# A first batch that is transposed on chip: an FFT filter and an MLP with ELU on one core

## The chip, the cores and the metric

The kernel runs on one core of a Trainium2 chip. The core has five engines that run side by side and wait for each other through semaphores: TensorE (PE in the profile; its weight loads are PEld), VectorE (DVE), ScalarE (ACT), GpSimd (POOL) and SyncE (SP), which only issues transfers here. Sixteen DMA engines move data between DRAM and the on-chip memory (SBUF); TensorE writes its results to a small memory of eight banks (PSUM), from which VectorE or ScalarE copies them. The metric is the device time of one execution in microseconds (us). Less is better.

## What is computed

Each of 8 batches of 3008 rows of 256 numbers goes through a real Fourier transform along the rows, is multiplied by a complex filter, and is transformed back. All rows then go through an MLP of width 2048 with ELU.

```python
X = np.fft.rfft(x, axis=1)                     # x: (8, 3008, 256) float32
y = np.fft.irfft(X * F[None], n=3008, axis=1)  # F = filt_r + 1j*filt_i, 1505 x 256
h = y.reshape(24064, 256) @ w_in               # 256 x 2048
g = np.where(h > 0, h, np.exp(np.minimum(h, 0)) - 1)
return g @ w_out                               # 2048 x 256
```

The weights w_in and w_out reach the kernel as 64-bit floats, 4.2 MB each, and are converted to 32-bit ones on the chip.

## The kernel before

3008 is 47 x 64, so the transform is made of two factors. Stage A contracts the 64 values of one index (with the pair n1 and 47 - n1 folded together), stage B the 47 values of the other. B's result is multiplied by the filter, and two more stages (Bi and N) go back. Then the MLP follows in items of one (batch, block m, quarter q), made with a Strassen-like scheme of 7 products up (w_in) and 7 down (w_out). Batches overlap: while the MLP of one batch fills TensorE, the transform of the next is slipped in. Only for the first batch there is no MLP to hide the transform behind. This is the part concerned.

Stage A leaves its rows in the wrong partitions for stage B. So its result t goes to a DRAM tensor z and comes back in another order.

```python
def x_unit(b, c):                 # c = 0..5: one block of 4 rows and their mirror rows
    nc.vector.tensor_tensor(out=u, in0=t[:, 0], in1=t[:, 1], op=ALU.add)
    nc.vector.tensor_tensor(out=t[:, 1], in0=t[:, 0], in1=t[:, 1], op=ALU.subtract)

def a_unit(b, c):                 # 16 matmuls of 64 x 64, two evictions
    ...
    nc.scalar.activation(out=t[:, 0:2, :], in_=p0, func=AXT.Copy)
    nc.scalar.activation(out=t[:, 2:4, :], in_=p1, func=AXT.Copy)

def z_write(b, c):                # 256 KB each, 1 KB runs
    ...
    for r in range(2):
        nc.sync.dma_start(z[r], t[HALVES[r]])

def z_read(b, g):                 # g = 0..7: one group of 4 frequencies
    for p, r in enumerate((0, 24, 64, 88)):
        nc.sync.dma_start(t[r:r + 24]..., zs[b][:, k:k + 4, :]...)
```

Stage B of a group, the product with the filter (the four VectorE lines are L251 to L254 of the profile), and stage Bi, whose result goes to DRAM (yd) and comes back for stage N:

```python
def b_unit(b, g, f=None):
    ...                                            # 4 matmuls of 512 columns
    nc.vector.tensor_tensor(out=sr, in0=re, in1=f[:, 0], op=ALU.mult)
    nc.vector.tensor_tensor(out=si, in0=re, in1=f[:, 1], op=ALU.mult)
    nc.vector.tensor_tensor(out=p, in0=im, in1=f[:, 1], op=ALU.mult)
    nc.vector.tensor_tensor(out=q, in0=im, in1=f[:, 0], op=ALU.mult)
    nc.gpsimd.tensor_tensor(out=sr, in0=sr, in1=p, op=ALU.subtract)
    nc.gpsimd.tensor_tensor(out=si, in0=si, in1=q, op=ALU.add)

def bi_unit(b, g):                                 # 4 matmuls, then two copies
    ...
    nc.scalar.activation(out=t[:, 0:2, :], in_=pa, func=AXT.Copy)
    nc.scalar.activation(out=t[:, 2:4, :], in_=pb, func=AXT.Copy)
```

The weights come in 16 pieces k (k = 4q + j; j = 0, 1 of w_in, j = 2, 3 of w_out), 0.5 MB each. A piece is fetched as pairs of 32-bit words and converted in one go: mantissa and exponent are taken apart, made floats, and joined.

```python
def w_convert(k):
    nc.vector.tensor_scalar(out=m, in0=hi, scalar1=0x000FFFFF, op0=ALU.bitwise_and, ...)
    nc.scalar.activation(out=l, in_=lo, func=AXT.Identity, scale=2.0 ** -52)
    nc.scalar.activation(out=f, in_=m, func=AXT.Identity, scale=2.0 ** -20, bias=1.0)
    nc.vector.tensor_scalar(out=e, in0=hi, scalar1=20, scalar2=0x7FF, ...)     # shift, and
    nc.vector.tensor_scalar(out=e, in0=e, scalar1=1151.0, scalar2=896.0, ...)  # min, max
    nc.vector.tensor_scalar(out=e, in0=e, scalar1=896.0, scalar2=8388608.0, ...)
    nc.vector.scalar_tensor_tensor(out=e, in0=hi, scalar=0x80000000, in1=e, ...)
    nc.vector.tensor_tensor(out=f, in0=f, in1=l, op=ALU.add)
    ... # one product (j < 2) or two half ones into the weight tile
    if j % 2 == 1:
        ... # four VectorE additions of 128 x 256 between the tile's blocks
```

The start, in program order:

```python
for c in range(NXC):                  # 6
    x_load(0, c, ...)                 # 6 (5 for c = 0) transfers on SP, one table on ACT
nc.gpsimd.memset(ff, 0.0)
... # tables; pieces 2 and 3
for a in range(2):
    f_read_first(ff, a)               # the filter of all groups, on GpSimd's queue
for c in range(NXC):
    x_unit(0, c); a_unit(0, c); z_write(0, c)
    if c in (0, 2): w_convert(c // 2)
for k in range(4, 7): w_fetch(k)
for k in range(2, 6): w_convert(k); w_fetch(k + 5)
z_read(0, 0); z_read(0, 1)
for g in range(NG + 2):               # 10
    if g >= 2: bi_unit(0, g - 2)
    if g < NG: b_unit(0, g, ff[:, g]); ...   # z_read(0, g + 2)
    if g >= 2: y_write(0, g - 2)
    if g in CONVERTS: w_convert(CONVERTS[g]) # {1: 6, 3: 7, 5: 8, 7: 9, 8: 10, 9: 11}
    ...
y_read(0, 0); w_convert(12)
... # fetch 13, 14, 15, each converted later between the first MLP items
n_unit(0, 0)
```

Of the kernel before, what the change touches and what calls it, by code (L numbers as in the profile page):

```python
# [10 lines left out]
FP32 = mybir.dt.float32  # L11
# [29 lines left out]
def _make_tables():  # L41
# [9 lines left out]

    n2, k2 = np.arange(N2), np.arange(K2)
    ta, tn = np.zeros((P, H, P)), np.zeros((P, H, P))
    for i in range(H):
        for h in range(2):
            if h and i == 0:
                continue
            n1 = N1 - i if h else i
            th = 2 * np.pi * (((N1 * n2[:, None] + n1) * k2[None]) % N) / N
            c, s = np.cos(th), -np.sin(th)  # L60
            c[:, 0], s[:, 0] = 1.0, 1.0 - 2.0 * (n2 % 2)
            sign = -1.0 if h else 1.0
            r = slice(h * 64, h * 64 + 64)
            for p, v in enumerate((c, sign * s, s, sign * c)):
                ta[r, i, p * 32:p * 32 + 32] = v
                tn[p * 32:p * 32 + 32, i, r] = v.T
    tb = ta.reshape(2, 2, 32, NXC, 2, 2, 4, 16, 2)[:, 0].transpose(3, 0, 1, 2, 4, 7, 5, 6)
# [24 lines left out]
    return [t.astype(np.float32) for t in (ta, tn, gb, gr, gi)]  # L92
# [8 lines left out]
def kernel(  # L101
# [11 lines left out]
    ta_d, tn_d, gb_d, gr_d, gi_d = [  # L113
        nc.inline_tensor(t, name=n).ap() for t, n in zip(_make_tables(), ("ta_t", "tn_t", "gb_t", "gr_t", "gi_t"))
# [28 lines left out]
    junk = glob.tile([P, 1], FP32, name="junk")  # L143
    fd = fdp.tile([NG, 2, 48, 2, 2, D], FP32, name="fd")
# [56 lines left out]

    def z_write(b, c):
# [18 lines left out]
    def f_read_first(t, a):  # L221
# [3 lines left out]
        for c, src in enumerate((filt_r, filt_i)):  # L225
            nc.gpsimd.dma_start(t[r:r + 24, :, c, :, :].rearrange("q g u d -> q g (u d)"),
                                raw(src, 2 * a, [[64 * D, 24], [4 * D, NG], [1, 2 * D]]))
            for u in range(2):
                g0 = 1 if a == u == 0 else 0
                for r0, n in ((24, 16), (40, 7)):  # L230
                    nc.gpsimd.dma_start(t[r + r0:r + r0 + n, g0:NG, c, u, :],
                                        raw(src, 64 * (r0 - 23) - 4 * g0 - 2 * a - u,
                                            [[64 * D, n], [-4 * D, NG - g0], [1, D]]))
            if a == 0:
                nc.gpsimd.dma_start(t[24:48, 0, c, 0, :], raw(src, 32, [[64 * D, 24], [1, D]]))
# [5 lines left out]
    def b_unit(b, g, f=None):  # L241
# [236 lines left out]
    wbufs = list(fbufs)  # L478

    def w_fetch(k):  # L480
        q, j = divmod(k, 4)

        wd = wds[k] = wbufs[k % 5 if k < 12 else (2, 0, 1, 2)[k - 12]].bitcast(U32).rearrange("p c u d -> p (c u d)").rearrange("p (a w) -> p a w", w=2)
# [8 lines left out]
    def w_convert(k):  # L492
# [3 lines left out]
        q, j = divmod(k, 4)  # L496
        if j < 2:
            dst = w_in[q][:, 2 * j:2 * j + 2, :, :].rearrange("p j a c -> p a j c")
            shape = dict(a=2, j=2)
        else:  # L500
            dst = w_out[q][:, 0:4, j - 2, :]
            shape = None
        wd = wds.pop(k)
        lo, hi = wd[:, :, 0], wd[:, :, 1]
        m, e = (kp.tile([P, 512], U32, tag=t, name=n) for t, n in (("k0", "wm"), ("k1", "we")))
        fl = kp.tile([P, 2, 512], FP32, tag="c", name="wfl")
        f, l = fl[:, 0], fl[:, 1]

        nc.vector.tensor_scalar(out=m, in0=hi, scalar1=0x000FFFFF, scalar2=None, op0=ALU.bitwise_and)
        nc.scalar.activation(out=l, in_=lo, func=AXT.Identity, scale=2.0 ** -52)  # L510
        nc.scalar.activation(out=f, in_=m, func=AXT.Identity, scale=2.0 ** -20, bias=1.0)

        nc.vector.tensor_scalar(out=e, in0=hi, scalar1=20, scalar2=0x7FF,
                                op0=ALU.logical_shift_right, op1=ALU.bitwise_and)
        nc.vector.tensor_scalar(out=e, in0=e, scalar1=1151.0, scalar2=896.0, op0=ALU.min, op1=ALU.max)
        nc.vector.tensor_scalar(out=e, in0=e, scalar1=896.0, scalar2=8388608.0,
                                op0=ALU.subtract, op1=ALU.mult)
        nc.vector.scalar_tensor_tensor(out=e, in0=hi, scalar=0x80000000, in1=e,
                                       op0=ALU.bitwise_and, op1=ALU.bitwise_or)
        nc.vector.tensor_tensor(out=f, in0=f, in1=l, op=ALU.add)  # L520
        if shape:
            f, e = (t.rearrange("p (a j c) -> p a j c", **shape) for t in (f, e.bitcast(FP32)))
        else:

            f, e = (t.rearrange("p (i a e s) -> p i e a s", i=2, a=4, e=2) for t in (f, e.bitcast(FP32)))
            dst = dst.rearrange("p (i e) (a s) -> p i e a s", i=2, a=4)
        if shape:
            nc.vector.tensor_tensor(out=dst, in0=f, in1=e, op=ALU.mult)
        else:
            for i in range(2):  # L530
                nc.vector.tensor_tensor(out=dst[:, i], in0=f[:, i], in1=e[:, i], op=ALU.mult)
        if j % 2 == 1:
            w = (w_in if j < 2 else w_out)[q]
            a11, a21, a12, a22, s1, s2, s4 = (w[:, i] for i in range(7))
            nc.vector.tensor_tensor(out=s1, in0=a21, in1=a22, op=ALU.add)
            nc.vector.tensor_tensor(out=s2, in0=s1, in1=a11, op=ALU.subtract)
            nc.vector.tensor_tensor(out=s4, in0=a12, in1=s2, op=ALU.subtract)
            nc.vector.tensor_tensor(out=a21, in0=a11, in1=a21, op=ALU.subtract)
# [19 lines left out]
    with tc.manual_schedule():  # L558


        CONVERTS = {1: 6, 3: 7, 5: 8, 7: 9, 8: 10, 9: 11}
        with tc.tile_pool(name="boot", bufs=1) as bp:
            ff = bp.tile([P, NG, 2, 2, D], FP32, name="ff")
            wbufs += [bp.tile([P, 2, 2, D], FP32, name="wb%d" % i) for i in range(2)]
            more = [(bp.tile([P, 2, 2, D], FP32, name="xb%d" % i), bp.tile([P, 2, P], FP32, name="tb%d" % i))
                    for i in range(NXC - XBUFS)]

            def wait_x(c):

                nc.gpsimd.tensor_copy(out=junk[0:1], in_=xs[0, c][0:1, 0, 0, 0:1])  # L570
# [3 lines left out]
            for c in range(NXC):  # L574
                x_load(0, c, nc.scalar, more[c - XBUFS] if c >= XBUFS else None)
            nc.gpsimd.memset(ff, 0.0)
            for t, d in ((gb, gb_d), (gr, gr_d), (gi, gi_d)):
                nc.gpsimd.dma_start(t, d)
            wait_x(3)
            w_fetch(2)  # L580
            w_fetch(3)
            wait_x(5)
            for a in range(2):
                f_read_first(ff, a)
            for c in range(NXC):
                x_unit(0, c)
                a_unit(0, c)
                z_write(0, c)
                if c in (0, 2):
                    w_convert(c // 2)  # L590
            for k in range(4, 7):
                w_fetch(k)
            for k in range(2, 6):
                w_convert(k)
                w_fetch(k + 5)
            z_read(0, 0)
            z_read(0, 1)
            for g in range(NG + 2):
                if g >= 2:
                    bi_unit(0, g - 2)  # L600
                if g < NG:
                    b_unit(0, g, ff[:, g])
                    if g + 2 < NG:
                        z_read(0, g + 2)
                if g >= 2:
                    y_write(0, g - 2)
                if g in CONVERTS:
                    w_convert(CONVERTS[g])
                if g == 1:
                    w_fetch(11)  # L610
                if g == 4:
                    w_fetch(12)
                if g in (5, 6):
                    x_load(1, g - 5)
# [4 lines left out]
        y_read(0, 0)  # L619
        w_convert(12)  # L620
        nc.gpsimd.tensor_copy(out=junk[0:1], in_=t4s[0, 0][0:1, 0, 0:1])
        for k in (13, 14, 15):
            w_fetch(k)
# [12 lines left out]
        for k in (13, 14, 15):  # L636
            at(max(k - 14, 0), 1, w_convert, k)
# [3 lines left out]
        for b in range(B):  # L641
            t = (b - 1) * PER
            if b > 0:
                for c, s in enumerate((0, 2, 3, 4, 6, 7)):
# [78 lines left out]
```

## Time and profile before

| | |
|---|---|
| time, median of 3 | 2698.39 us (2697.93 to 2698.43) |
| profiled span | 2697.7 us |
| PE busy | 2593.4 us, 96% |
| DVE busy | 1870.0 us, 69% |
| ACT busy | 1474.7 us, 55% |
| POOL busy | 279.9 us, 10% |
| mean granted TensorE clock | 0.977 |

The profile is one execution. Its page has busy times by engine, the span in 40 slices with the busy share of each in tenths, the chain of work that ended last (followed back from the last instruction, at each step to what released it), and groups of instructions by line and tile. Busy time of TensorE overstates its work where matmuls are pipelined. The trace behind the page can be asked for a stretch: busy time of each engine, granted clock, DMA share and GB/s.

The groups of the MLP fill most of the span; columns here are line, engine, operation, tiles and shape, count | busy us, mean ns | idle before.

```profile
L426 PE MATMUL po<-g,wo 128*128 128x256 f32 (+1 forms) x5376 | 1298.1, 376 | 0.0
L344 PE MATMUL phs<-y,wi 128*128 128x256 f32 (+1 forms) x1536 | 395.5, 380 | 0.0
L256 POOL TENSOR_TENSOR sr<-sr,sp 128x512 f32<-128x512 f32 x64 | 81.2, 1269 | 1265.3 <-DVE sp L253 1265.3
```

### The profile page before, as it was taken

The page shows a single profiled execution, that of the slowest core. Times are in us where ns is not written, and L with a number is a line of the kernel's source. Part 1 is how long each engine was busy: PE and PEld are TensorE (multiplying, and loading weights), DVE is VectorE, ACT ScalarE, POOL GpSimd, SP SyncE. Part 2 cuts the span into 40 slices and gives each one's busy share as a digit, 9 for nine tenths or more (in the row PEclk, how much of TensorE's full clock was granted, in tenths as well). Part 3 has the DMA queues.
Part 4 walks back from the last instruction along what each step waited for, and adds up shares of the span by engine and source line. Part 5 has one row for each costly group of instructions (what it writes and reads, how often), then busy time and mean ns, then how long its engine had stood idle before and what let it go on. Part 6 is the DMA issues. An engine that isn't in the chain of part 4 may idle for free.

```text
span 2697.7 us, 37154 instructions
## 1 busy us (share of the span) xinstructions
PE 2593.4 (96%) x13376; PEld 2196.4 (81%) x13376; DVE 1870.0 (69%) x3243; ACT 1474.7 (55%) x2561; POOL 279.9 (10%) x325
## 2 busy tenths in 40 slices
PE   1689999999999999999999999999999999999998
PEld 1278888987889878988889887898789888899887
DVE  4876776667667677767766677676767767666665
ACT  2255555555556555555555555565556555555554
POOL 4311210002100120001200021000210012000000
PEclk7589999999999999999999999999999999999999
DMA  9545331434213431153314332143421233110010
GB/s 232 156 121 132 79 78 40 101 77 104 62 38 89 103 96 38 45 124 79 85 37 91 90 90 70 38 101 83 114 58 38 60 87 92 38 40 19 21 27 16
DMA packets 234934, 208.23 MB, mean 77 GB/s; under 512 B 134052, under 2 KB 201142, under 8 KB 234752
## 3 DMA queue, kind: packets, MB, share of 16 engines
q1 hardware_dynamic: 216096, 168.15, 25.3%
q0 software_dynamic: 17792, 36.93, 5.6%
q8 instruction: 106, 1.74, 0.3%
q10 hardware_dynamic: 864, 0.79, 0.1%
q14 instruction: 76, 0.62, 0.1%
HBM read 130.68 MB, written 78.12 MB: 77 GB/s over the span
## 4 chain that ended last, share of the span: by engine, by line
PE 94%; DMA 2%; DVE 2%; issue 1%; SPq 0%; ACT 0%; POOL 0%; ACTq 0%; DVEq 0%; POOLq 0%
PE po L426 42%; PE phs L344 25%; PE phd L344 12%; PE pha L344 6%; PE psn L296 3%; PE pva L239 2%; PE psr L239 2%; PE psa L194 2%; DMA z<-t 0%; DMA ff<-in_filt_i_dram 0%; DMA ta<-ta_t 0%; PE pvb L239 0%; SPq L176 0%; DMA t<-z 0%; DMA xb<-in_x_dram 0%
## 5 line engine op out<-in xcount | busy, mean ns | idle before, releaser
L426 PE MATMUL po<-g,wo 128*128 128x256 f32 (+1 forms) x5376 | 1298.1, 376 | 0.0
L426 PEld LDWEIGHTS po<-g,wo 128*128 128x128 f32 x5376 | 1016.3, 190 | 129.4 <-issue 15.4
L355 ACT ACTIVATE g<-phs 128x512 f32<-128x512 f32 (+1 forms) x576 | 339.0, 589 | 845.3 <-PE phs L344 844.6
L352 DVE TENSOR_TENSOR g<-phd,g 128x512 f32<-128x512 f32 (+1 forms) x384 | 259.6, 676 | 462.8 <-ACT e L362 277.8
L362 ACT ACTIVATE e<-e 128x512 f32<-128x512 f32 (+1 forms) x768 | 477.3, 622 | 24.4
L344 PE MATMUL phs<-ys,wi 128*128 128x256 f32 (+1 forms) x1536 | 388.9, 376 | 11.2 <-ACT g L355 11.2
L344 PE MATMUL phs<-y,wi 128*128 128x256 f32 (+1 forms) x1536 | 395.5, 380 | 0.0
L366 DVE SCALAR_TENSOR_TENSOR g<-e,g 128x512 f32<-128x512 f32 (+1 forms) x576 | 387.2, 672 | 0.0
L361 ACT ACTIVATE e<-g 128x512 f32<-128x512 f32 (+1 forms) x576 | 352.8, 613 | 36.7 <-DVE g L352 30.6
L344 PEld LDWEIGHTS phs<-y,wi 128*128 128x128 f32 x1536 | 285.1, 190 | 82.9 <-ACT t L267 34.1
L344 PEld LDWEIGHTS phs<-ys,wi 128*128 128x128 f32 x1536 | 292.4, 191 | 45.4 <-ACT g L355 12.3
L366 DVE SCALAR_TENSOR_TENSOR g<-e,phs 128x512 f32<-128x512 f32 (+1 forms) x192 | 130.0, 677 | 139.6 <-ACT e L362 139.6
L256 POOL TENSOR_TENSOR sr<-sr,sp 128x512 f32<-128x512 f32 x64 | 81.2, 1269 | 1265.3 <-DVE sp L253 1265.3
L344 PE MATMUL phd<-ys,wi 128*128 128x256 f32 (+1 forms) x768 | 193.9, 375 | 1.8 <-DVE g L352 1.8
L344 PE MATMUL pha<-y,wi 128*128 128x256 f32 (+1 forms) x768 | 194.0, 375 | 0.0
L344 PE MATMUL phd<-y,wi 128*128 128x256 f32 (+1 forms) x768 | 193.9, 375 | 0.0
L361 ACT ACTIVATE e<-phs 128x512 f32<-128x512 f32 (+1 forms) x192 | 113.0, 588 | 140.5 <-PE phs L344 139.6
L344 PEld LDWEIGHTS phd<-ys,wi 128*128 128x128 f32 x768 | 145.7, 190 | 19.0 <-DVE g L352 2.6
L344 PEld LDWEIGHTS pha<-y,wi 128*128 128x128 f32 x768 | 146.3, 191 | 16.6
L344 PEld LDWEIGHTS phd<-y,wi 128*128 128x128 f32 x768 | 145.7, 190 | 17.2 <-issue 0.4
L406 DVE TENSOR_TENSOR g<-g,g 128x512 f32<-128x512 f32 (+1 forms) x192 | 130.7, 681 | 6.7
L403 DVE TENSOR_TENSOR g<-g,g 128x512 f32<-128x512 f32 (+1 forms) x192 | 130.7, 681 | 6.6
(111 smaller groups left out, 2377.6 us busy)
## 6 DMA issues: line engine op xcount, KB each, us to landing
z<-t SPq DMA_DIRECT2D x96, 256.0 KB
t<-z SPq DMA_DIRECT2D x256, 96.0 KB
yd<-t SPq DMA_DIRECT2D x128, 192.0 KB
t<-yd SPq DMA_DIRECT2D x192, 128.0 KB
f<-fd POOLq DMA_DIRECT2D x112, 192.0 KB, 3.7
out_dram<-o SPq DMA_DIRECT2D x640, 32.0 KB
tn<-tn_t SPq DMA_DIRECT2D x48, 256.0 KB
xc<-in_x_dram SPq DMA_DIRECT2D x92, 128.0 KB
```

The source lines that it names most:

```text
L239: nc.tensor.matmul(ps[:, u:u + w, :], table[k, v, :], rhs[k, u:u + w, :], start=True, stop=True)
L256: nc.gpsimd.tensor_tensor(out=sr, in0=sr, in1=p, op=ALU.subtract)
L296: nc.tensor.matmul(ps[:, ts(q, P)], t[:, i - 4 * m, ds(dh * P, P)], w[:, i - 4 * m, :], start=True, stop=True)
L344: nc.tensor.matmul(ps[:, a, 0:h], w_in[q][:, COMBO[n], a, :], y[n], start=start and a == 0, stop=True, skip_group_check=True)
L352: nc.vector.tensor_tensor(out=g[o], in0=i0, in1=i1, op=ALU.add)
L355: nc.scalar.activation(out=g[o], in_=i0, func=AXT.Copy)
L361: nc.scalar.activation(out=e, in_=src, func=AXT.Relu, scale=-1.0)
L362: nc.scalar.activation(out=e, in_=e, func=AXT.Exp, scale=-1.0)
L366: nc.vector.scalar_tensor_tensor(out=g[n], in0=es[n], scalar=1.0, in1=src, op0=ALU.subtract, op1=ALU.max)
L403: nc.vector.tensor_tensor(out=b12, in0=b22, in1=b12, op=ALU.subtract)
L406: nc.vector.tensor_tensor(out=g["t4"], in0=g["b21"], in1=g["t2"], op=ALU.subtract)
L426: nc.tensor.matmul(po[i][:, u, 0:h], w_out[q][:, COMBO[n], a, :], g[n][:, a, :], start=q == 0 and a == 0 and n in (1, 3, 6, 4), stop=True, ...
```

## The change

For the first batch only, the way from stage A to stage B no longer goes through DRAM. Stage A is turned round: x is the stationary operand and the table the moving one, so that the channels come to lie on the partitions. The result is copied, strided, into tiles that later hold the weights of quarters 2 and 3 (`zt`); TensorE then transposes them, 128 x 112 at a time, against an identity matrix, and ScalarE copies the transposes to where stage B reads. The sum and difference of x_unit fall away, as a table of full height (`tf`) holds both. It is meant to take the round trip through z off the start, and the bytes with it.

The conversion of a weight piece is cut into four steps that are spread over three engines and two turns of the loop: `w_split` (VectorE), `w_float` (ScalarE, which now also clamps the exponent), `w_sum` (GpSimd) and `w_join` (VectorE; for j = 1 the four additions of the tile's blocks on GpSimd). All 16 pieces are converted before the first N stage. The filter is read on SP's queue instead of GpSimd's, and ff is zeroed by ScalarE.

```diff
+    def a_first(c):
+        for dh in range(2):
+            k, ps = bank("psa", (P, 64, XC, 2))
+            for u in range(XC):
+                nc.tensor.matmul(ps[:, :, u, :], xt[:, u, ts(dh, P)], w[:, u, :]..., ...)
+            for kh in range(2):
+                ... # o: strided view of zt[kh][dh], s: half of ps
+                if dh: nc.vector.tensor_copy(out=o, in_=s)
+                else:  nc.scalar.activation(out=o, in_=s, func=AXT.Copy)
+
+    def t_first(g):
+        for j in range(2):
+            ps = psO.tile([P, 2, 256], FP32, name="po%d" % i)
+            for u in range(2):
+                k = 4 * g + 2 * j + u
+                for dh in range(2):
+                    nc.tensor.transpose(ps[0:ROWS, u, ts(dh, P)], zt[k // 16][dh][:, ts(k % 16, ROWS)], eye)
+            nc.scalar.activation(out=t[0:ROWS, 2 * j:2 * j + 2, :], in_=ps[0:ROWS], func=AXT.Copy)
...
-            nc.gpsimd.dma_start(t[r:r + 24, :, c, :, :]...          # f_read_first, all its reads
+            nc.sync.dma_start(t[r:r + 24, :, c, :, :]...
...
+    W_PLACE = (0, 1, 2, 3, 4, 5, 6, 3, 4, 5, 6, 0, 1, 2, 0, 1)      # buffer of each piece
+    def w_split(k):
+        nc.vector.tensor_scalar(out=m, in0=hi, scalar1=0x000FFFFF, ...)
+        nc.vector.tensor_scalar(out=e, in0=hi, scalar1=0x7FF00000, ...)
+    def w_float(k):
+        nc.scalar.activation(out=l, in_=wds[k][:, :, 0], func=AXT.Identity, scale=2.0 ** -52)
+        nc.scalar.activation(out=f, in_=m, func=AXT.Identity, scale=2.0 ** -20, bias=1.0)
+        nc.scalar.activation(out=ef, in_=e, func=AXT.Relu, scale=-8.0, bias=edges[:, 0:1])
+        nc.scalar.activation(out=e, in_=ef, func=AXT.Relu, scale=-1.0, bias=edges[:, 1:2])
+    def w_sum(k):
+        nc.gpsimd.tensor_tensor(out=f, in0=f, in1=l, op=ALU.add)
+    def w_join(k):
+        nc.vector.scalar_tensor_tensor(out=e, in0=hi, scalar=0x80000000, in1=e, ...)
+        ... # product(s) into the weight tile, as before
+        if j % 2 == 1:
+            eng = nc.gpsimd if j == 1 else nc.vector
+            ... # the four additions, on eng
...
+        FETCH = {0: 8, 1: 9, 2: 10, 3: 11, 4: 12, 5: 13, 7: 14, 8: 15}
+            for k in range(2): w_fetch(k)
+            for c in range(NXC): x_load_first(c)       # two transfers on SP, a table on ACT
+            nc.scalar.memzero(ff)
+            for t, d in ((gb, gb_d), (gr, gr_d), (gi, gi_d), (gf, gf_d), (eye, eye_d)):
+                nc.scalar.dma_start(t, d)
+            for a in range(2): f_read_first(ff, a)
+            for c in range(NXC):
+                w_split(c)
+                if c > 0: w_sum(c - 1)
+                nc.gpsimd.tensor_copy(out=junk[0:1], in_=xs[0, c][0:1, 0, 0:1])   # waits for x
+                w_fetch(c + 2)
+                a_first(c)
+                w_float(c)
+                if c > 0: w_join(c - 1)
+            t_first(0)
             for g in range(NG + 2):
+                k = NXC + g
+                w_split(k); w_sum(k - 1)
+                if g + 1 < NG: t_first(g + 1)
                 if g >= 2: bi_unit(0, g - 2)
-                if g < NG: b_unit(0, g, ff[:, g]); ...
+                if g < NG: b_unit(0, g, ff[:, g], gf)
                 if g >= 2: y_write(0, g - 2)
-                if g in CONVERTS: w_convert(CONVERTS[g])
+                w_float(k); w_join(k - 1)
+                if g in FETCH: w_fetch(FETCH[g])
         y_read(0, 0)
-        w_convert(12)
+        w_sum(15); w_join(15)
+        for c in range(2): x_load(1, c)
...
-        for k in (13, 14, 15):
-            at(max(k - 14, 0), 1, w_convert, k)
-                for c, s in enumerate((0, 2, 3, 4, 6, 7)):
+                for c, s in enumerate((1 if b == 1 else 0, 2, 3, 4, 6, 7)):
```

## The prediction

> **What bounds the kernel now.** I read first the page's forty slices (67.4 us each; tenths of busy time).
>
> ```profile
> PE   1689999999999999999999999999999999999998
> DVE  4876776667667677767766677676767767666665
> PEclk7589999999999999999999999999999999999999
> ```
>
> From the fourth slice on TensorE is full. TensorE is busy for 2593.4 of 2697.7 us, so about 104 us stand idle, nearly all in the first three slices. The diff leaves the 190 or so items after the start alone (one x unit moves by a step). So the change is worth what it does to the start, us for us, and can't bring much over 100.
>
> Second, the stretches of 20 us. Columns: stretch, length, busy us (and instructions) of PE, PEld, DVE, ACT, POOL, then granted clock, DMA share, GB/s.
>
> ```profile
> 20.00:40.00 20.00, 9.77 (x80) 6.79 (x80) 13.57 (x26) 4.32 (x8) 8.46 (x16) 0.83 0.97 226
> 40.00:60.00 20.00, 0.00 (x0) 0.00 (x0) 6.65 (x15) 4.43 (x8) 10.27 (x18) 0.52 1.06 244
> 60.00:80.00 20.00, 11.09 (x41) 4.56 (x42) 16.09 (x28) 4.40 (x8) 7.32 (x8) 0.50 0.73 223
> 80.00:100.00 20.00, 13.86 (x47) 3.70 (x48) 17.20 (x31) 5.16 (x10) 7.08 (x7) 0.50 0.50 145
> 100.00:120.00 20.00, 16.11 (x53) 4.28 (x51) 15.88 (x23) 4.84 (x9) 10.66 (x10) 0.50 0.62 168
> 120.00:140.00 20.00, 7.25 (x28) 5.94 (x25) 18.21 (x40) 6.38 (x11) 3.12 (x6) 0.51 0.67 182
> 140.00:160.00 20.00, 9.96 (x55) 7.99 (x54) 15.36 (x31) 9.39 (x18) 0.00 (x0) 0.83 0.56 141
> ```
>
> Three regimes: up to 60 us the DMA engines are full and compute waits; from 60 to 120 us VectorE is 79 to 86% busy while TensorE runs at half clock; from 120 to 160 us VectorE is busy with weights while TensorE mostly waits.
>
> Third, the chain of work that ended last (start, length, what).
>
> ```profile
> 33.13 11.07 DMA ff<-in_filt_i_dram
> 44.49 2.23 DMA ff<-in_filt_r_dram
> 46.72 0.56 ACT wfl L510
> 47.36 13.09 DMA z<-t
> 61.16 6.42 DMA t<-z
> 67.71 1.94 PE psr L239 x4
> ...
> 126.11 2.63 DMA yd<-t
> 129.11 0.76 SPq L283
> 130.37 3.40 DMA t<-yd
> 133.91 3.76 PE psn L296 x16
> ```
>
> The round trip through z, 13.09 + 6.42 us, is on the path and ends last before the B stage. The z writes shared their time with the filter reads.
>
> **What the Trainium skill says.** (1) "DMA: Bandwidth & Descriptors", section "Queues, rings and completion order": each DMA engine goes round its queues packet by packet. So bytes on one queue slow another. The trace agrees: z<-t, 256 KB, took 13.09 us in a stretch whose DMA share is 1.06. (2) "TensorE: Matmul & The Clock Gate", Part 1: an idle TensorE gets half its clock, and sustained work brings it back. The trace agrees on 0.50 from 60 to 120 us and 1.00 when full, though the B stage at 70 to 80% busy did not raise it. (3) The same page, Part 4: transposes don't count as work for the clock; and Part 1 gives 107 ns from one 128-column matmul to the next when cold. No run here shows either for a transpose yet; I take the clock to stay at 0.5. (4) "SBUF — State Buffer", "Who interferes with whom": some VectorE operations lock out, or are locked out by, GpSimd. The trace agrees: the 0.42 us bit operation took 1.11 and 1.49 us (at 116.90 and 117.93) beside the GpSimd add of 1.27 us.
>
> **The change, part by part.** Four milestones in the trace before: first product with the filter (VectorE, L251) at 72.4 us; last such product ends at 117.0; the four additions behind the first N matmuls end at 139.4; TensorE is full from about 158.
>
> *Up to the first product.* It needs ff whole and group 0 of B. Removed: 3.1 MB written to z and the first reads of it. Added: the full-height table, 1.57 MB where 0.79 was. Bytes wanted by then: x 3.1, table 1.6, ff 3.1, other tables 0.3, and weight pieces 0 to 5 at 0.52 each, 3.1: 11.2 MB. The stretches give 192 GB/s in the first 20 us (3.8 MB) and 226 to 244 after; 7.4 MB at 235 are 31 us, so ff lands near 51.
>
> ScalarE has a chain of its own. Its small table loads wait in its queue for earlier transfers, by the built program's list of waits as late as one of x block 3, so I put its first copy at about 22 us. Then six rounds of two strided copies (estimate 0.45 us each, half an eviction of 0.59) and four conversions at 0.63 (groups, L511: 627 ns): 3.4 us, hence 22 + 20.5 = 42.5. Two copies of transposes (0.59 each) and the B matmuls (2 to 3 us cold): 47. Pieces are fetched one round after GpSimd's sum, so the weights may add 3 us. The two paths tie; I take 50. Before: 72.4. **Gain 22 us.**
>
> *The eight groups.* Before, b and bi of a group, back to back, took 4.6 us of cold TensorE (84.41 to 89.00), and a group took (117.0 - 72.4)/7 = 6.4 us with its last. Now TensorE also transposes: eight of 128 columns. A cold 512-column float matmul leaves two records 0.91 us apart (pva at 86.30 and 87.21). If a transpose is one pass at one column a cycle, the page's 107 ns hold for it: 0.85 us a group, an estimate. b of the next group can't begin before the products of this one end, nor before the transposes and bi; with bi at 2.3 and b at 2.7, the sum is 0.85 + 2.3 + 2.7 = 5.9 us. VectorE per group: products 2.5 (four, 0.60 us apart and 0.68 long at 114.50 to 116.98), join 0.69 + 0.7, split 0.84 plus about 0.6 in which GpSimd holds it, and four additions, 1.7, every fourth piece: 5.8. A conversion on VectorE falls from eight operations (0.42 x 4 + 0.69 x 4 = 4.4; one piece at 108 to 121 us shows the same lengths) to four (2.2), but now each of the eight groups converts a piece, where four of them did (groups 1, 3, 5 and 7). ScalarE: 4 x 0.59 + 4 x 0.63 = 4.9. GpSimd: 2 x 1.27 + 1.27 + 1 + a share of sums: 5.5. Everything fits near 6.0. Seven periods and a last product of 2.5 make 44.5; with the usual slips 45 us, against 44.6. **Gain 0.** I don't expect the lighter VectorE to show here.
>
> *From the last product to the first N.* Before 22.4 us (117.0 to 139.4). Now, with T the end of the last product: piece 14 is fetched only after the last two GpSimd sums, issued at T+3.1, landed at T+7 (median landings of 3.7 us for 192 KB without rivals), split and four ScalarE operations end at T+9.8. The copies of the last bi stand behind those in ScalarE's order: T+11. Write 2.6 and read 3.4 plus issues: N matmuls at T+18. Piece 15 is issued behind GpSimd's four additions for piece 13 (4 x 0.65, estimate from 1.27 for twice the size), lands at T+17, and its conversion and four additions stand in front of N's four on VectorE: these end at T+24.6. **Loss 2 us.**
>
> *After N.* Before, pieces 13 to 15 were converted between the first MLP items: TensorE did 0.68, 0 and 1.95 us in the three 4 us stretches from 148 to 160, at half clock at the end, and stood 1.2 us at 172. All weights are now ready: I count 10 of those 12 us back, less 1 for item 0's own chain. The 1.5 us at 212 (memset of f) stays. **Gain 9 us.**
>
> Sum: 22 + 0 - 2 + 9 = 29 us; 2698.4 - 29 = 2669, rounded up to **2670 us**.
>
> **Rivals.**
> 1. *ScalarE or the weights become the bound of the start.* ScalarE was busy 5 us of 20; it now makes four conversions a piece and all the copies, in program order, and each piece waits on a fetch. For: GpSimd's order of fetches, and the copies of the last bi behind piece 14. Against: 4.9 of 6.0 us per group. If so, 10 us more at the two ends: 2680.
> 2. *The transposes cost four cycles a column, as float matmuls do.* Four times 0.85 is 3.4 us a group, 2.55 more, on the path: 7 x 2.55 = 18 us; 2688. For: no row shows a transpose. Against: the built program has a single instruction for each.
> 3. *TensorE warms up.* b, bi and transposes at full clock: the group then is VectorE's, 5.5 us, and contention is less; 5 to 8 us better, and a faster front (46) brings 2658. Against: 0.50 all through 60 to 120 us.
> 4. *The transfers were hidden anyway*, ff being the bound either way: the chain shows ff landing at 46.7 before, and z after it; so z's 20 us are truly on the path.
>
> **Range and chances.** The front is uncertain by 5 us, the groups by +18/-6, the tail by 6. Eight in ten: **2655 to 2690 us**. 2% is 54 us, below 2644.4: it would need all of the four to go well (0.05). 2% slower needs a loss where about 20 us of transfers vanish (0.01). Within 2%: 0.94.
>
> **What would show it.** Right: first product at 46 to 56 us; eight groups over about 45 us at clock 0.5; first N matmul near 113, its additions' end near 120; no hole of TensorE as from 148 to 158. Wrong: first product after 60; transposes of about 0.4 us apart; groups below 5 us; ScalarE idle on a weight fetch for more than 10 us in the tail.

## The result, and the profile after

| | before | after |
|---|---|---|
| time, median | 2698.41 us | 2699.07 us |
| profiled span | 2697.7 us | 2696.9 us |
| end of the first group's four products with the filter | 74.85 us | 65.99 us |
| end of the last group's | 116.98 us | 126.10 us |
| end of the four N additions | 139.39 us | 151.90 us |

The ratio of after to before is 1.0001 (95% interval 0.9983 to 1.0018): no change. The table's steps say where the gain went. The front became 8.9 us shorter (prediction: 22, for the start of the first product, which went from 72.4 to 60.5). The eight groups took 60.1 us instead of 42.1 (prediction: no change). From the last product to the end of the additions it is 25.8 us instead of 22.4. The N additions thus end 12.5 us later, and yet the span is 0.8 us shorter, so 13.3 us were won behind them (prediction: 9).

The forty slices of after, to compare with the three lines of before:

```profile
PE   4689999999999999999999999999999999999998
...
DVE  3957776667667676767766677676767767666665
...
PEclk7689999999999999999999999999999999999999
```

VectorE's second slice went from 8 to 9: that is where the groups lie. The stretches of 20 us of after (columns as before):

```profile
20.00:40.00 20.00, 11.94 (x68) 10.95 (x67) 9.71 (x17) 12.56 (x26) 12.15 (x18) 0.83 1.07 203
40.00:60.00 20.00, 7.67 (x52) 5.52 (x52) 9.63 (x19) 12.02 (x21) 4.42 (x5) 0.67 0.86 146
60.00:80.00 20.00, 10.32 (x36) 4.04 (x36) 16.38 (x17) 4.23 (x8) 11.98 (x12) 0.56 0.31 85
80.00:100.00 20.00, 14.20 (x50) 5.11 (x50) 19.69 (x27) 11.64 (x21) 10.66 (x11) 0.66 0.34 93
100.00:120.00 20.00, 14.29 (x53) 4.63 (x54) 19.69 (x21) 10.30 (x19) 15.20 (x15) 0.63 0.38 107
120.00:140.00 20.00, 5.30 (x14) 0.65 (x8) 10.92 (x17) 6.43 (x11) 11.48 (x13) 0.50 0.33 94
140.00:160.00 20.00, 12.27 (x56) 10.70 (x56) 13.29 (x27) 10.03 (x18) 1.79 (x2) 0.76 0.89 210
```

From 80 to 120 us VectorE is busy 19.69 of 20 us with 27 and 21 instructions, where it had 31 and 23 in 17.20 and 15.88 us: fewer instructions, more busy time. So each got longer. The chain of work that ended last, in after:

```profile
26.33 11.43 DMA ff<-in_filt_r_dram
37.78 19.13 DMA ff<-in_filt_r_dram
56.92 7.06 DMA ff<-in_filt_i_dram
...
72.55 6.30 DVE we L590
...
84.18 3.69 DVE wo L602 x2
...
107.00 6.30 DVE we L590
...
137.95 6.00 DMA f<-in_moe_w_out_dram
```

Three parts can be read off: up to 64 us the filter's reads (no z any more); in the groups, VectorE's join (L590 sets the sign, L596 and L602 multiply the factors); at the end, a weight piece that is fetched late.

How long the join's instructions are in the groups (60 to 130 us; count | busy us, mean ns | idle before):

```profile
L590 DVE SCALAR_TENSOR_TENSOR we<-wb,we 128x512 uint32<-128x512 uint32 x6 | 18.3, 3042 | 0.0
...
L602 DVE TENSOR_TENSOR wo<-wfl,we 128x256 f32<-128x256 f32 x8 | 7.9, 1027 | 0.4
L596 DVE TENSOR_TENSOR wi<-wfl,we 128x512 f32<-128x512 f32 x4 | 6.3, 1570 | 0.4
L312 DVE TENSOR_TENSOR sr<-psr,ff 128x512 f32<-128x512 f32 x8 | 5.5, 683 | 9.0 <-DMA ff<-in_filt_r_dram 9.0
```

L590 took 3042 ns in the mean of these six (and 1384 in the mean of two on another buffer), where the same operation took 0.69 us in the groups of before:

```profile
L518 DVE SCALAR_TENSOR_TENSOR we<-f,we 128x512 uint32<-128x512 uint32 x2 | 1.4, 693 | 0.1
```

The product with the filter, one of whose operands is in PSUM, kept its 0.68 us, although the fourth one (L315) ran beside a GpSimd addition in all eight groups. And this is what runs beside the longest of them (VectorE, then GpSimd; start, length):

```profile
72.48 6.37 DVE L590 SCALAR_TENSOR_TENSOR we<-wb,we 128x512 uint32<-128x512 uint32 x1
78.95 0.76 DVE L602 TENSOR_TENSOR wo<-wfl,we 128x256 f32<-128x256 f32 x2
```

```profile
72.75 1.28 POOL L584 TENSOR_TENSOR wfl<-wfl 128x512 f32<-128x512 f32 x1
73.98 1.26 POOL L317 TENSOR_TENSOR sr<-sr,sp 128x512 f32<-128x512 f32 x1
75.20 1.26 POOL L318 TENSOR_TENSOR si<-si,sq 128x512 f32<-128x512 f32 x1
76.41 0.57 POOL L552 DMA_DIRECT2D wb<-in_moe_w_in_dram  x1
77.01 1.28 POOL L584 TENSOR_TENSOR wfl<-wfl 128x512 f32<-128x512 f32 x1
```

One VectorE instruction lasts from 72.48 to 78.85 us; GpSimd's last addition ends at 78.29. VectorE gets through when GpSimd stops.

### The profile page after: what moved, and what is told of

Same layout as the page of the kernel before. It is cut to its first block, busy times and chain, and to the rows that moved or that the text cites. A ratio compares the mean times of both kernels' runs of the same rounds, so it can differ in the third digit from the quotient of the medians.

```text
span 2696.9 us, 37188 instructions
## 1 busy us (share of the span) xinstructions
PE 2605.7 (97%) x13440; PEld 2210.1 (82%) x13440; DVE 1859.5 (69%) x3181; ACT 1507.5 (56%) x2610; POOL 294.2 (11%) x338
## 4 chain that ended last, share of the span: by engine, by line
PE 93%; DVE 3%; DMA 3%; issue 0%; POOL 0%; ACT 0%; SPq 0%; DVEq 0%; POOLq 0%
PE po L487 42%; PE phs L405 24%; PE phd L405 12%; PE pha L405 6%; PE psn L357 3%; PE pva L300 2%; PE psr L300 2%; PE psa L201 2%; DMA ff<-in_filt_r_dram 1%; DVE we L590 1%; DMA t<-tf_t 1%; DVE wo L602 0%; DMA f<-in_moe_w_out_dram 0%; DMA ff<-in_filt_i_dram 0%; DMA gr<-gr_t 0%
```

## Theories

**A.** GpSimd's additions hold off those VectorE instructions that read two operands from SBUF; the change gave GpSimd more of them and VectorE had no idle time left. **B.** The groups are bound by a cold TensorE that now also transposes. **C.** The front is late because the filter's reads moved to SP's queue or are narrow. **D.** What cost time in the groups is the wait of VectorE or TensorE for GpSimd's results, a dependency and not an interference.

## Experiments

In each, the ratio is to the kernel before, with its 95% interval. The diffs are cut to the lines that carry the change. "Front" is the end of the first group's products, "groups" from there to the end of the last group's, "tail" from there to the end of the N additions.

**1. The weight sums on VectorE** (GpSimd keeps the complex product's two additions)

```diff
-        nc.gpsimd.tensor_tensor(out=f, in0=f, in1=l, op=ALU.add)
+        nc.vector.tensor_tensor(out=f, in0=f, in1=l, op=ALU.add)
-            eng = nc.gpsimd if j == 1 else nc.vector
+            eng = nc.vector
```

> Only the sums of the conversion and the four additions of pieces with j = 1 go back from GpSimd to VectorE. Theory A (GpSimd's work blocks VectorE operations with two operands in SBUF; the sign-and-exponent join took 1.4 to 6.4 us where it takes 0.69 alone): the eight groups, from the end of the first group's products to the end of the last one's, fall from 60 us to 46 to 50, although VectorE gets more to do; time 2686 to 2690. Theory B (cold TensorE with transposes, B and Bi is the bound): the groups stay at 58 to 62 us, time 2697 to 2700.

Measured: 2689.1 us, 0.9962 (0.9949 to 0.9975); front 66.6, groups 53.7, tail 22.6. Work was added to the engine that was full, and the groups became 6.4 us shorter. That speaks for A. B can't make it: TensorE's work is the same. A's 46 to 50 us was missed, as the complex product's two additions still ran beside the join: L590 took 1.38 us beside them.

**2. Queues exchanged** (1, and the filter's reads on GpSimd's queue as before, pieces from the third on SP's)

```diff
-            nc.sync.dma_start(t[r:r + 24, :, c, :, :]...    # all reads of the filter
+            nc.gpsimd.dma_start(t[r:r + 24, :, c, :, :]...
-            nc.gpsimd.dma_start(wd[:, ts(i, n), :]..., s)
+            (nc.gpsimd if k < 2 else nc.sync).dma_start(wd[:, ts(i, n), :]..., s)
```

> As the run with the sums on VectorE, and the filter reads go back to GpSimd's queue while weight pieces 2 to 15 go to SP's. Theory C (narrow filter reads on SP's queue are what brings ff late, at 64 us): the first group's products end at 50 to 56 us instead of 66, and the time falls by another 8 to 12 us below the run with the sums alone. Rival (the bytes bound the start wherever they are queued): products end at 62 to 67 us, and the two runs are within 3 us.

Measured: 2694.85 us, 0.9983 (0.9975 to 0.999); front 75.0, groups 53.7, tail 19.3. Both expectations missed. The last read of the filter landed at 55.2 us (64.0 in after), but the third weight piece only at 52.1, and the pieces' conversion stands ahead of the transposes in program order. The exchange moved the lateness from the filter to the weights: the queues decide which bytes come late. As both moved at once, the run doesn't show what SP's queue alone costs the filter; but a mere exchange of queues doesn't bring the first product forward.

**3. Pieces 14 and 15 fetched earlier** (after, nothing else)

```diff
-    W_PLACE = (0, 1, 2, 3, 4, 5, 6, 3, 4, 5, 6, 0, 1, 2, 0, 1)
+    W_PLACE = (0, 1, 2, 3, 4, 5, 6, 3, 4, 5, 6, 0, 1, 2, 3, 0)
-        FETCH = {..., 7: 14, 8: 15}
+        FETCH = {..., 6: 14, 7: 15}
```

> Only the place and the turn of fetching pieces 14 and 15 change: each is fetched one turn earlier (14 into a buffer free since group 2, 15 into piece 11's). If the fetch of these pieces holds the last Bi copies and the first N (25.8 us from the last product to the end of the first N's additions), this falls to 16 to 19 us and the time to 2689 to 2692. If the end is held by the engines' own work, it stays above 23 us and the time within 2 us of 2699.

Measured: 2695.3 us, 0.9986 (0.9979 to 0.9993); front 65.6, groups 61.1, tail 20.9. In after, VectorE waited 3.14 us for piece 14 and 9.68 us for piece 15; these waits are gone, and the tail is 4.9 us shorter. That lies between the two expectations: other waits took their place, such as one of 2.5 us for a GpSimd sum.

**4. All three edits** (1, 2 and 3 in one; one line each of 3 and 2 is shown)

```diff
+    W_PLACE = (0, 1, 2, 3, 4, 5, 6, 3, 4, 5, 6, 0, 1, 2, 3, 0)
+            (nc.gpsimd if k < 2 else nc.sync).dma_start(wd[:, ts(i, n), :]..., s)
```

> All three edits. If the three causes are separate, the gains add: about 11 (groups), 10 (start) and 8 (tail) give 2667 to 2673. If one bound stands behind all of them, the sum falls short: above 2680.

Measured: 2695.16 us, 0.9986 (0.9979 to 0.9993); front 75.1, groups 53.7, tail 19.5. The gains don't add: the front's loss of 2 (9.1 us) takes back most of what the other two edits give (12.8).

**5. The filter in wide reads.** 24 reads are replaced by 4 of the same bytes, in runs of 16 KB. The filter's values then stand in other places, so the output isn't the reference's; only the form of the transfer is measured.

```diff
+            nc.sync.dma_start(t[r:r + 48, :, c, :, :].rearrange("q g u d -> q g (u d)"),
+                              raw(src, 737 * a, [[16 * D, 48], [2 * D, NG], [1, 2 * D]]))
```

> The changed kernel with the 24 filter reads replaced by four of the same bytes in all, each 48 partitions of 16 KB that lie together in DRAM; the filter's values land in the wrong places, so the output isn't the reference's. If the shape of the reads (7, 16 and 24 partitions, runs of 1 and 2 KB a long way apart, eight transfers under way at most) makes ff late, the first group's products end at 50 to 56 us instead of 66. If bytes alone bound the start, they end at 62 us or later.

Measured: 2693.33 us, 0.9981 (0.9974 to 0.9988); front 60.7, groups 60.1, tail 26.4. The form of the reads is worth 5.2 us of the front, and those pass on to the end. Both expectations missed (50 to 56; 62 or later): the form is a part of the delay, and this run doesn't show what the rest is.

**6. No arithmetic on GpSimd in the first batch** (1, and the complex product's additions on VectorE too)

```diff
-        nc.gpsimd.tensor_tensor(out=sr, in0=sr, in1=p, op=ALU.subtract)
-        nc.gpsimd.tensor_tensor(out=si, in0=si, in1=q, op=ALU.add)
+        eng = nc.vector if b == 0 else nc.gpsimd
+        eng.tensor_tensor(out=sr, in0=sr, in1=p, op=ALU.subtract)
+        eng.tensor_tensor(out=si, in0=si, in1=q, op=ALU.add)
```

> The sums of the conversion, the four additions, and for the first batch the two sums behind the filter products are all on VectorE; GpSimd only issues fetches in the groups. If GpSimd's arithmetic is what stretches VectorE's operations with two operands in SBUF, the join's first operation takes 0.69 us every time and its product 0.69 or 0.42; the groups stay near the 53.7 us of the run with the sums alone, since VectorE takes over 1.4 us a group and loses about 1.6 of waiting. If the join is slow by itself (bit operation, operands), it stays at 1.3 us or more and the groups rise to 60 or more.

Measured: 2683.44 us, 0.9948 (0.9933 to 0.9963); front 67.0, groups 50.5, tail 19.4. VectorE now does all of it, and the groups are 9.6 us shorter than in after. The same groups of instructions, again from 60 to 130 us:

```profile
L585 DVE TENSOR_TENSOR wfl<-wfl 128x512 f32<-128x512 f32 x10 | 6.8, 683 | 0.0
...
L603 DVE TENSOR_TENSOR wo<-wfl,we 128x256 f32<-128x256 f32 x12 | 4.6, 422 | 0.2
...
L591 DVE SCALAR_TENSOR_TENSOR we<-wb,we 128x512 uint32<-128x512 uint32 x6 | 4.1, 681 | 0.0
L597 DVE TENSOR_TENSOR wi<-wfl,we 128x512 f32<-128x512 f32 x5 | 3.5, 693 | 0.2
```

3042 ns became 681, 1570 became 693, 1027 became 422. The sum that took GpSimd 1.30 us takes VectorE 0.68. VectorE is busy 59.1 of the 60 us from 70 to 130: full, now with its own work. GpSimd still issues the fetches of weights in these groups, and nothing gets longer: it is its additions that lengthen.

**7. Pieces 12 to 15 converted between the first MLP items** (1, with these pieces moved behind N, as before did with 13 to 15)

```diff
+        for i, k in enumerate((12, 13, 14, 15)):
+            at(i, 0, w_split, k); at(i, 0, w_float, k); at(i, 1, w_sum, k); at(i, 1, w_join, k)
```

> As the run with the sums on VectorE, and pieces 12 to 15 are converted in the first four MLP items (split and conversion in the middle of an item, sum and join at its end). If VectorE's load before N is now the bound, the N additions end at 129 to 134 us (143 with the sums alone) and the time is 2677 to 2684. If converting beside the MLP costs as much there, the time stays at 2687 or more.

Measured: 2694.49 us, 0.9991 (0.9982 to 0.9999); front 65.1, groups 51.8, tail 17.5. N's additions end at 134.3 us, 8.6 earlier than in 1, and the time is 5.4 us longer: TensorE is busy 43.8 of the 50 us from 180 to 230, against 48.2 in 1. Among its waits in the MLP is one of 3.1 us for a weight product (L602). From the end of N's additions to the end of the run it is 2556.8 us, against 2545.6 in 1; in before it was 2558.3, in after 2545.0. So having all weights ready before N is worth 11 of the 13 us.

**8. The transposes alone** (the kernel before, with stage A turned round and transposed on chip; conversion, its places and all queues as before)

```diff
-                x_unit(0, c); a_unit(0, c); z_write(0, c)
+                a_first(c)
-            z_read(0, 0); z_read(0, 1)
+            t_first(0)
-                    b_unit(0, g, ff[:, g])          # and z_read(0, g + 2)
+                    b_unit(0, g, ff[:, g], gf)      # and t_first(g + 1) at the loop's head
```

> The kernel before with the transposes on chip alone: conversion in one go and its places, filter reads and fetches on GpSimd's queue all as before. If the trip through DRAM was on the path, the first group's products end at 58 to 64 us (74.9 before), the groups take the 42 to 45 us of before, and the time is 2683 to 2689. If the start is bound by something that the trip only hid, the products end at 70 us or later and the time is 2695 or more.

Measured: 2693.59 us, 0.9985 (0.9978 to 0.9992); front 69.0, groups 42.0, tail 22.0. All transposes lie in these groups too, and the groups are as short as before: B falls. On its own this half of the change brings 5.8 us in the front and 4.1 at the end, between the two expectations. From its chain (start, length, what):

```profile
49.77 7.74 DMA wb<-in_moe_w_in_dram
57.53 0.43 DVE wm L570
...
66.55 0.68 DVE sr L312
```

With z gone, the first product waits for weight piece 4, whose fetch stands behind the filter's reads in GpSimd's queue, and for the conversion of pieces 4 and 5 on VectorE, which stands ahead of the product in program order (57.5 to 66.3 us).

**9. The filter in two parts** (6, with the reads for groups 0 and 1 ahead of those for 2 to 7)

```diff
-            for a in range(2):
-                f_read_first(ff, a)
+            for ga, gb_ in ((0, 2), (2, 8)):
+                for a in range(2):
+                    f_read_first(ff, a, ga, gb_)
```

> The version without GpSimd sums in the first batch (2683.4 us), in which the filter's reads come in two parts: groups 0 and 1 first, then groups 2 to 7. Theory F (the first product waits for bytes that only the later groups need): the first group's products end near 57 instead of 67.0 us, and because VectorE then starts the groups 10 us earlier and is the bound until their end, the N additions end some 6 to 9 us earlier than 136.9 and the time is 2674 to 2678. Rival G (VectorE's conversions only move from before the first product into the groups; weight pieces land late because the bytes before 60 us are the same): the first product is earlier, but the groups get longer by as much, time 2681 to 2684.

Measured: 2680.83 us, 0.9936 (0.9924 to 0.9949); front 48.4, groups 65.1, tail 19.1. The front is 18.6 us earlier than in 6, and the end only 2.6 us (0.9936 against 0.9948; the intervals overlap). What VectorE then waited for in groups 2 and on (total us, times, longest):

```profile
DVE si L314 <- DMA ff<-in_filt_i_dram: 7.3, 1, 7.3
DVE sr L313 <- DMA ff<-in_filt_r_dram: 7.1, 1, 7.1
```

The rest of the filter landed at 75.3 us, later than the whole of it in 6. Neither F (2674 to 2678) nor G (2681 to 2684) alone: the first product no longer waits for other groups' bytes, but the bytes themselves are as many as in 6.

**10. GpSimd adds for nobody** (6, with two additions per group on GpSimd whose result is never read)

```diff
                     b_unit(0, g, ff[:, g], gf)
+                    for i in range(2):
+                        nc.gpsimd.tensor_tensor(out=idle, in0=ff[:, g, 0], in1=ff[:, g, 1], op=ALU.add)
```

> The version without GpSimd sums in the first batch (2683.4 us), with two additions per group put on GpSimd (128x512, both operands in SBUF, the filter's two halves) whose result nobody reads. No engine waits for them. Theory A (GpSimd's reading of SBUF holds off VectorE's instructions with two SBUF operands): VectorE's additions, sign instruction and products of factors in the groups take up to 2 us instead of 0.68, the eight groups take 58 to 66 us instead of 50.5, time 2690 to 2698. Rival H (what GpSimd cost was the wait of the next engine for its result, a dependency): nothing waits, so all instructions keep 0.68 and the time stays within 2 us of 2683.

Measured: 2696.85 us, 0.9995 (0.9987 to 1.0003); front 64.4, groups 65.5, tail 19.0. No engine waits for these additions, and the groups are 15.0 us longer than in 6 (they start 2.6 us earlier, and the last product ends 12.4 us later). VectorE is idle for 0.7 us of the groups in both runs. D falls: with nothing to wait for, it costs as much, all of it in the length of VectorE's instructions. VectorE in two groups of this run; GpSimd's last addition ended at 96.83 us:

```profile
86.51 1.36 DVE L318 TENSOR_TENSOR sr<-sr,sp 128x512 f32<-128x512 f32 x1
87.80 1.88 DVE L319 TENSOR_TENSOR si<-si,sq 128x512 f32<-128x512 f32 x1
89.60 1.75 DVE L591 SCALAR_TENSOR_TENSOR we<-wb,we 128x512 uint32<-128x512 uint32 x1
91.39 2.92 DVE L603 TENSOR_TENSOR wo<-wfl,we 128x256 f32<-128x256 f32 x2
...
98.49 0.68 DVE L585 TENSOR_TENSOR wfl<-wfl 128x512 f32<-128x512 f32 x1
...
101.49 0.69 DVE L318 TENSOR_TENSOR sr<-sr,sp 128x512 f32<-128x512 f32 x1
102.08 0.69 DVE L319 TENSOR_TENSOR si<-si,sq 128x512 f32<-128x512 f32 x1
102.69 0.69 DVE L591 SCALAR_TENSOR_TENSOR we<-wb,we 128x512 uint32<-128x512 uint32 x1
```

The same lines take 1.36 to 1.88 us while GpSimd adds and 0.69 once it has stopped.

**11. The conversion alone** (the kernel before, with the four steps in place of its conversion, at its places; sum and join one piece later). One thing differs from the reference: the scratch tiles of the second piece are taken again by stage A before its join, so some weights get other values.

```diff
+    def w_convert(k):
+        w_split(k); w_sum(k - 1); w_float(k); w_join(k - 1)   # pieces 12 to 15 in one go
-                if g == 1: w_fetch(11)
-                if g == 4: w_fetch(12)
+                if g in (1, 3, 5): w_fetch(10 + g // 2)
```

> The kernel before, with its data through DRAM and its places, in which only the conversion is replaced by the new four steps (split, floats, sum on GpSimd, join one piece later). Theory A: the six conversions in the groups add GpSimd work of 1.3 us and more each beside VectorE's two-operand instructions; with VectorE's own work per piece 1.3 us less, the groups take 44 to 50 us instead of 42.1 and the time is 2699 to 2706. Rival (fewer VectorE instructions help where VectorE was 80% busy): groups at 42 or less, and 2694 to 2698. With the transposes alone at 2693.6 and both at 2699, the two parts would add up if this is near 2703.

Measured: 2708.74 us, 1.0044 (1.003 to 1.0057); front 81.8, groups 40.9, tail 22.5. Both expectations missed. The groups are no longer, although the lengthening is there: L526, the sign, took 1258 ns in the mean from one buffer and 950 from the other (60 to 130 us). But only three conversions fall between the two ends, as in before, and VectorE, with fewer instructions per piece, had room: it is idle for 7.7 of the 40.9 us. The loss is in the front, 7.0 us, and behind N, 2.0. GpSimd's first sum starts at 54.0 us, behind the last of the filter's reads in the same queue, and VectorE is busy for 5.1 of the 40 us from 20 to 60 (20.2 in before). That this is what makes the front late is argued and not tested.

**12. All that helped, in one** (the edits of 6, 9 and 3)

```diff
+        eng = nc.vector if b == 0 else nc.gpsimd
+            for ga, gb_ in ((0, 2), (2, 8)):
+    W_PLACE = (0, 1, 2, 3, 4, 5, 6, 3, 4, 5, 6, 0, 1, 2, 3, 0)
```

> All that has helped, in one: no GpSimd sums in the first batch, the filter in two parts, pieces 14 and 15 of the weights fetched one group earlier into buffers that are free sooner. Under theory F 2670 to 2676 us; under rival G 2679 to 2683 us, as the early fetch takes 2 to 4 us from the end of the groups to the N additions at most.

Measured: 2676.92 us, 0.9927 (0.9914 to 0.9939); front 49.0, groups 61.8, tail 19.2. N's additions end at 130.0 us, 21.8 earlier than in after; the time is 22.2 us shorter than after's. It lies between F's range and G's.

```profile
40.00:60.00 20.00, 14.07 (x76) 8.29 (x77) 17.23 (x35) 12.46 (x22) 2.04 (x4) 0.67 0.91 153
60.00:80.00 20.00, 9.41 (x37) 3.28 (x35) 8.75 (x19) 5.42 (x11) 3.49 (x7) 0.50 0.86 205
80.00:100.00 20.00, 14.82 (x68) 5.24 (x64) 19.79 (x39) 12.84 (x24) 0.00 (x0) 0.76 0.23 60
100.00:120.00 20.00, 7.77 (x27) 2.19 (x24) 19.66 (x40) 12.22 (x21) 1.58 (x3) 0.50 0.33 90
```

VectorE does 39 and 40 instructions in the 40 us in which it did 27 and 21 in after. What is left: VectorE full from 80 to 120 us, more than half idle from 60 to 80, where it waits for the rest of the filter at a DMA share of 0.86.

**The groups taken apart.** VectorE's time from the end of the first group's products to the end of the last group's, from the traces: what its instructions take with no GpSimd addition beside them, what they took beyond that, and its idle time (us):

| run | undisturbed | lengthening | idle | sum |
|---|---|---|---|---|
| before | 29.4 | 5.6 | 7.1 | 42.1 |
| after | 33.9 | 25.3 | 0.9 | 60.1 |
| 1, weight sums on VectorE | 41.3 | 11.8 | 0.7 | 53.7 |
| 6, no GpSimd additions | 49.7 | 0.1 | 0.7 | 50.5 |
| 10, as 6, GpSimd adds for nobody | 49.7 | 15.2 | 0.7 | 65.6 |
| 12, all that helped | 49.8 | 0.2 | 11.8 | 61.8 |

## Why the prediction was wrong

*"The eight groups. Gain 0": failed, and it decides the case.* I summed VectorE's work per group as "join 0.69 + 0.7, split 0.84 plus about 0.6 in which GpSimd holds it", 5.8 us in all, which fitted into a period of 6.0. I let GpSimd hold off only the split, because in before's groups that is where it does; the join was put in at full speed. In before the join had come after GpSimd's additions; in after it comes right behind the four products, when GpSimd starts. By the table above, each of the seven periods took 8.6 us: 4.8 undisturbed, 3.6 of lengthening instead of my 0.6, and 0.1 idle. Of the 25.3 us of lengthening the join has 22.4 (L590 14.9, L602 4.9, L596 2.6) and the split 2.8; before's 5.6 us are all in the bit operations and the clamp of the old conversion. The growth of 18.0 us is 19.7 more lengthening and 4.5 more work (seven conversions instead of three), less 6.2 of idle time that before still had. Experiments 6 and 10 show the cause itself. (My 4.4 us for a conversion of before should have been 3.8 by the lengths in the trace; nothing hung on it.)

I had cited the Trainium skill, "SBUF — State Buffer", section "Who interferes with whom", and then didn't go through my own list of VectorE instructions with it: it says that a VectorE instruction with two SBUF inputs contends with a GpSimd one that reads SBUF, which is all of the join and none of the products with PSUM. The runs agree: 0.69 to 3.04 us, and 0.68 unchanged. Theory A as I put it is too narrow, though: the split's bit operations have one operand in SBUF and were held as well (0.42 us to as much as 2.16 in after). And the trace of before shows the hold on two SBUF operands too, outside the part that I read. One addition of the MLP, L442, takes 0.39 to 0.43 us with no GpSimd addition beside it and 1.37 us each of the 14 times that one ran there (VectorE, then GpSimd, one of these times), while before's fourth product with the filter (L254), always beside one, took 0.68 in all 64 groups:

```profile
386.05 1.37 DVE L442 TENSOR_TENSOR c<-c,k 128x256 f32<-128x256 f32 x1
```

```profile
385.67 1.46 POOL L257 TENSOR_TENSOR si<-si,sq 128x512 f32<-128x512 f32 x1
```

*"Up to the first product. Gain 22 us": direction right, term mis-sized: 11.9 us.* "ff lands near 51" was 64.0. I counted six weight pieces; `w_fetch(c + 2)` fetches eight in that loop, 1.0 MB more, so 12.2 MB, and the trace has 12.3 by 66 us. And "226 to 244" GB/s did not hold: 203 from 20 to 40 us, 146 from 40 to 60. Before's rate had z's writes in it; without them the rate fell. So taking bytes away freed less time than their share. Part of the low rate is the form of the filter's reads (5.2 us, experiment 5); why the rest is slow stays open. The other half of this step was right: ScalarE's chain and TensorE can be ready near 47, as experiment 9 shows (without GpSimd's additions), whose first product starts at 45.9 as soon as the bytes come in the right order.

I had also misread what stood beside z in before. The "46.7" in the chain is the landing of one of the filter's 22 reads. They were issued until 51.1 us, and the last landed at 60.0:

```profile
L231 POOL DMA_DIRECT2D ff<-in_filt_i_dram x8: 547/577/699, 33.8 to 51.1; - x8
```

So z, at 67.6, ended only 7.6 us behind the filter, and behind z VectorE was converting pieces 4 and 5 until 70.4, 2 us ahead of the first product. Little of z's 20 us stood alone on the path.

*"From the last product to the first N. Loss 2 us": right in kind, 3.4 measured.* Piece 15 was the last link, as predicted (VectorE waited 9.68 us for it); with its early fetch (experiment 3) the tail is 20.9 us, under before's 22.4.

*"After N. Gain 9 us": right in kind, 13.3 measured.* The hole moved up with everything else and the first items run without it; experiment 7 gives it back when the pieces are moved there again.

*The rivals.* The first (ScalarE or the weights) came in the tail only. The second (slow transposes): in part; each is one record, but they came every 0.21 us at half clock, twice the estimate, and they were not on the path: the groups of experiment 8 took 42.0 us with them. The third (TensorE warms up) came true in part, granted clock 0.56 to 0.66 instead of 0.50 in the groups, and brought nothing, as VectorE was the bound. The fourth (transfers hidden anyway), which I dismissed with the misread 46.7, was nearly true: experiment 8 has z gone and wins 4.1 us of the 20, with its filter at 56.4 us and the weights behind it. The range did give the groups "+18", with transposes in mind, but for the front only 5 us of doubt, where 10 to 13 were missing; the two together lie outside it.

## What to carry over

Moving work to an idle engine pays only if that engine leaves the full one alone: go through the full engine's instructions one by one, note where each operand lies, and ask which of them can run beside the helper. Here 16 additions of 1.3 us on the helper cost VectorE 15.2 us in experiment 10, 0.95 each, more than the 0.68 us that it would have needed itself. And when a transfer disappears, ask what ended close behind it (in experiment 8 two weight pieces took z's place), and which bytes the first waiter truly needs: order of arrival was worth 18.6 us of the front, but it is won at the end only if the bytes behind it arrive in time.

## What the runs showed of the hardware

- The hold is not of one instruction's length. In after, one L590 lasted 6.37 us beside four GpSimd additions with a transfer's issue among them; in experiment 10, where VectorE met GpSimd pair by pair, 1.36 to 1.88. What makes the one wait through several and the other get in between was not tested.
- A transpose of 128 columns, against the identity, came every 0.21 us at granted clock 0.50, not 0.107 as I estimated from the Trainium skill, "TensorE: Matmul & The Clock Gate", Part 1, whose figure is of bf16 matmuls, while these are of float32: 1.7 us a group. The lines are of after:

```profile
74.86 0.42 PE L257 MATMUL po<-eye,wo 128*112 128x128 f32 x1
75.07 0.42 PE L257 MATMUL po<-eye,wi 128*112 128x128 f32 x1
75.28 0.42 PE L257 MATMUL po<-eye,wo 128*112 128x128 f32 x1
```

- The granted clock is not bound to 0.50 in such a start: in after it was 1.00 from 52 to 53 us, with transposes and B's first matmuls, and the transposes then lay some 0.11 us apart.
